# Split operands for the first two batches and ten slots of a fused attention and feed-forward kernel, other homes for batch 1's raw keys and values, another order of the first steps

## The chip, the cores and the metric

The kernel runs on one core of one Trainium2 chip. The metric is device time in microseconds (us) of the whole program; a result is the median over runs. About 0.2% (3.6 us) is what a measurement of this kernel can tell from no change.

The engines by their names in the profile: PE (TensorE, matmuls; PEld its weight loads), DVE (VectorE), ACT (ScalarE), POOL (GpSimd), SP (SyncE, here only a queue that issues DMA transfers).

## The reference

Three stages follow one another. Eight batches, eight heads, 576 rows, head dimension 64; 4608 tokens of width 512; hidden widths 2048 and 1536.

```python
k_p = k.reshape(B, H, 72, 8, D).mean(axis=3)
v_p = v.reshape(B, H, 72, 8, D).mean(axis=3)
scores = (1 / sqrt(D)) * q @ k_p.T
attn = softmax(scores)
x = attn @ v_p
h = x @ w_in
x = (h * cos(h)) @ w_out
out = (silu(x @ w_gate) * (x @ w_val)) @ w_out2
```

## The kernel before, in words

**Order of the work.** Attention for batch 0 comes first, as a written-out list of steps (`program`, line 1083). Then 9 blocks of 512 tokens go through the second stage in 16 slots each (a slot is 128 hidden columns); the steps of batches 1 to 7 are hung on those slots by hand (`START`, `MID`, `LATE`, `EXP`, `NORM`, lines 412 to 425). The third stage follows from about 995 us on and is not touched. A scheduler of the framework takes the instructions in priority of program order, by its own model of time, and lets later ones go ahead where earlier ones are not ready; on the chip each engine then runs its list strictly in that order.

**Number formats.** An fp32 matmul is one instruction that the trace shows as two records. The other form, fp32r, needs each operand as a high and a low part: the high part is made by a copy on ACT, the low part by a subtraction on DVE, and the product is hi\*hi + hi\*lo + lo\*hi, three matmuls. `ACTB = 2` (line 67) and `Y32 = NF1` = 16 (line 68) say where plain fp32 is used: for batches 0 and 1 in the attention product (`do_av`, line 375), and for all 16 slots of block 0 in the second product of the second stage (`pe_y`, line 591).

**Attention, per tile of 128 rows.** `do_qt` transposes q on PE; `do_s` (298) makes scores into two PSUM banks of the tag `att`, the minima on DVE (312) and the exponentials on ACT (318); `do_norm` (330) scales into `pm` on DVE (343, 350); `do_pt` (354) transposes `pm` on PE into an `att` bank and copies it to SBUF (363, 366); `do_av` multiplies with v, four head pairs per group of tiles, into `att` banks, and ACT moves the result into `ring` (399). The tag `att` has two banks. For batches 2 to 7 `do_pt` also makes low parts on DVE (369, 373), `do_norm` a copy of the leftover columns (352), `prep_v` the low parts of v (267 to 280), and `do_av` has five products per head pair in place of two.

**Weights.** All weights arrive as 64-bit numbers and are turned into fp32 by ACT (477) and three DVE operations (482, 487, 494); `w_in` pieces ("i", 16 of them) are split as well (1010, 994). `conv` (979) does it in a fixed list, the 8 first pieces of `w_in`, then `w_out` pieces ("o", 16) in turn with the other 8; `fill(m)` takes m steps from it. `load_i` and `load_o` issue the loads on SP's queue; o pieces pass through a ring of two buffers, i pieces land where the finished piece will be (`wa..`).

**Second stage, per slot.** `pe_h` (531): 12 matmuls of 512 columns. `turns` and `cosine` (542, 565): two DVE operations, three on ACT. `pe_y`: four fp32 matmuls, or 12 fp32r matmuls; for the latter `parts` (575) makes the split of the result (584, 587) and, in blocks 0 and 1, that of the `w_out` piece (553, 586).

**Raw keys and values.** Those of batch 1 (`load_kv1`, 189) go to places of later `w_in` pieces (tags `wa30` to `wa32`, `wa20` to `wa22`), are added up by DVE (steps K0, K1, K2, U0), and the loads of those pieces wait on SP's queue until then. Those of later batches are added up by POOL.

Of the kernel before, what the change touches and what calls it, by code (L numbers as in the profile page):

```python
# [8 lines left out]
F32 = mybir.dt.float32  # L9
F32R = mybir.dt.float32r  # L10
# [15 lines left out]
def fused_kernel(  # L26
# [18 lines left out]
    nc = tc.nc  # L45
    B, H, S, D = q.shape
# [3 lines left out]
    P = 128  # L50
    POOL = 8
    SP = S // POOL
    NP = H // 2
    SM = 64
    SL = SP - SM
    TB = 512
    NB = NT // TB
    KC = DM // P
    NF1 = FF1 // P
# [5 lines left out]
    PTW = 320  # L65
    LEAD = 4
    ACTB = 2
    Y32 = NF1

    const = ctx.enter_context(tc.tile_pool(name="const", bufs=1))  # L70
    chain = ctx.enter_context(tc.tile_pool(name="chain", bufs=2))
# [12 lines left out]
    mask = few[:, 0]  # L84
# [20 lines left out]
    kT = p1a.tile([P, NP, 2 * SP], F32, name="kT")  # L105
    av_tiles = {}

    def av_tile(nm, b):

        kind = F32 if b < ACTB else F32R  # L110
        if (nm, kind) not in av_tiles:
            shape = {"v": [P, NP, P], "p": [P, NP, PTW], "x": [P, PTW]}["x" if nm == "ptx" else nm[0]]
            t = av_tiles[nm, kind] = p1a.tile(shape, kind, name=f"{nm}_{b}", tag=nm)
            if nm in ("vmh", "vml", "vl2"):
                nc.gpsimd.memset(t if kind is F32 else t.bitcast(F32), 0.0)
        return av_tiles[nm, kind]

    nc.gpsimd.memset(kT, 0.0)
    for nm in ("vmh", "vml", "vl1", "vl2", "pth", "ptl", "ptx"):
        av_tile(nm, 0)  # L120

    def raw_tile(nm):
        return chain.tile([P, 2, TB], F32, name=nm, tag="raw", bufs=2)
# [64 lines left out]

    def load_kv1():

        for g in range(3):
            t = wts.tile([P, 2, TB], F32, name=f"k1_{g}", tag=f"wa3{g}")
            kraw1.append(t if g < 2 else t[: SL * NP])
            if g < 2:
                for x in range(2):
                    nc.sync.dma_start(t[x * SM : (x + 1) * SM], kview[1][g, x])
            else:
                for r in range(2):
                    nc.sync.dma_start(t[: SL * NP, r], kleft[1][r])
        for j in range(0, NP + 1, 2):  # L200
            t = wts.tile([P, 2, TB], F32, name=f"v1_{j}", tag=f"wa2{j // 2}")
            for r in range(2):
                rows = t[r * SM : (r + 1) * SM]
                if j < NP:
                    nc.sync.dma_start(rows, vview[1][r, :, j : j + 2])
                else:
                    nc.sync.dma_start(rows[:, 0], vleft[1])
            vraw1.append((j, t[:, : min(2, NP + 1 - j)]))

    def pool_sum(eng, dst, raw):  # L210
        h = POOL * D // 2
# [37 lines left out]
            nc.scalar.mul(to[:, :, SM:], ps[rows, 2 * P :].rearrange("d (s p) -> d p s", p=NP), -EXP_SCALE)  # L249

    def prep_v(b):
        vmh, vml, vl1, vl2 = (av_tile(nm, b) for nm in ("vmh", "vml", "vl1", "vl2"))
        vp = vps.pop(b)
        if b < ACTB:
            for r in range(2):
                rows, cols = slice(r * SM, (r + 1) * SM), slice(r * D, (r + 1) * D)
                nc.scalar.mul(vmh[rows, :, cols], vp[rows, :NP], 1.0 / POOL)
            nc.vector.tensor_mul(
                vl1[:SM].rearrange("q p (r d) -> q r p d", r=2),
                vp[:SM, NP : NP + 1].rearrange("q (a o) d -> q a o d", a=1).to_broadcast([SM, 2, NP, D]),  # L260
                mask[:SM].rearrange("q (p r o) -> q r p o", r=2, o=1).to_broadcast([SM, 2, NP, D]),
            )
            return
        for r in range(2):
            rows, cols = slice(r * SM, (r + 1) * SM), slice(r * D, (r + 1) * D)
            nc.scalar.mul(vmh[rows, :, cols], vp[rows, :NP], 1.0 / POOL)
            nc.vector.scalar_tensor_tensor(
                out=vml[rows, :, cols], in0=vp[rows, :NP], scalar=1.0 / POOL, in1=vmh[rows, :, cols],
                op0=ALU.mult, op1=ALU.subtract,
            )  # L270
        t = p1a.tile([P, H, SP], F32, name=f"vt_{b}", tag="e")[:, :, :D]
        nc.vector.tensor_mul(
            t, vp[:, NP : NP + 1].to_broadcast([P, H, D]), mask.rearrange("p (h o) -> p h o", o=1).to_broadcast([P, H, D])
        )
        t = t.rearrange("q (p r) d -> q r p d", r=2)
        h2 = vl1.rearrange("q p (r d) -> q r p d", r=2)
        l2 = vl2.rearrange("q p (r d) -> q r p d", r=2)
        for r in range(2):
            nc.scalar.copy(h2[:, r], t[:, r])
            nc.vector.tensor_sub(l2[:SM, r], t[:SM, r], h2[:SM, r])  # L280
# [49 lines left out]
    def do_norm(b, t, pm=None):  # L330
        n = TILES[t][1]
        e = es.pop((b, t))[:n]
        if b < ACTB:
            sm = sms.pop((b, t))[:n]
        else:
            sm = p1a.tile([P, H, 1], F32, name=f"sm_{b}_{t}", tag="sm", bufs=2)[:n]
            nc.vector.reduce_sum(sm[:, :, 0], e, axis=AX.X)
        nc.vector.tensor_scalar_add(sm, sm, 1e-9)
        nc.vector.reciprocal(sm, sm)
        if pm is None:  # L340
            pm = p1a.tile([P, H * SM + P], F32, name=f"pm_{b}_{t}", tag="pm")
        pms[b, t] = pm
        nc.vector.tensor_mul(
            pm[:n, : H * SM].rearrange("q (h s) -> q h s", h=H), e[:, :, :SM], sm.to_broadcast([n, H, SM])
        )

        for g in range(2):
            left = pm[:n, H * SM + g * SM : H * SM + (g + 1) * SM].rearrange("q (h s) -> q h s", h=H)
            if g == 0:
                nc.vector.tensor_mul(left, e[:, :, SM:], sm.to_broadcast([n, H, SL]))  # L350
            elif b >= ACTB:
                nc.vector.tensor_copy(pm[:n, H * SM + SM :], pm[:n, H * SM : H * SM + SM])

    def do_pt(b, t):
        pth, ptl, ptx = av_tile("pth", b), av_tile("ptl", b), av_tile("ptx", b)
        t0, n = TILES[t]
        o = t0 - GROUPS[GROUP[t]][0]
        pm = pms.pop((b, t))
        ps = psum.tile([P, NP, n], F32, name=f"pt_{b}_{t}", tag="att", bufs=2)
        for p in range(NP):  # L360
            pinned(nc.tensor.transpose(ps[:, p], pm[:n, p * P : (p + 1) * P], ident[:n, :n]), (b, t) == (0, 4))
        if b < ACTB:
            nc.scalar.copy(pth[:, :, o : o + n], ps)
            px = psum.tile([SM, n], F32, name=f"px_{b}_{t}", tag="att", bufs=2)
            nc.tensor.transpose(px, pm[:n, NP * P : NP * P + SM], ident[:n, :n])
            nc.scalar.copy(ptx[:SM, o : o + n], px)
            return
        nc.scalar.copy(pth[:, :, o : o + n], ps)
        nc.vector.tensor_sub(ptl[:, :, o : o + n], ps, pth[:, :, o : o + n])
        px = psum.tile([P, n], F32, name=f"px_{b}_{t}", tag="att", bufs=2)  # L370
        nc.tensor.transpose(px, pm[:n, NP * P :], ident[:n, :n])
        nc.scalar.copy(ptx[:, o : o + n], px)
        nc.vector.tensor_sub(ptx[SM:, o : o + n], px[SM:], ptx[SM:, o : o + n])

    def do_av(b, g, p):
        vmh, vml, vl1, vl2, pth, ptl, ptx = (
            av_tile(nm, b) for nm in ("vmh", "vml", "vl1", "vl2", "pth", "ptl", "ptx")
        )
        g0, n = (GROUPS if b else GROUPS0)[g]
        o = 256 if g == 2 else 0  # L380
        ps = psum.tile([P, n], F32, name=f"av_{b}_{g}_{p}", tag="att", bufs=2)
        terms = [
            (vmh, pth[:, p, o : o + n]),
            (vmh, ptl[:, p, o : o + n]),
            (vml, pth[:, p, o : o + n]),
            (vl1, ptx[:, o : o + n]),
            (vl2, ptx[:, o : o + n]),
        ]
        if b < ACTB:
            terms = [(vmh, pth[:, p, o : o + n])]  # L390
            terms += [(vl1[:SM], ptx[:SM, o : o + n])]
        for i, (w, x) in enumerate(terms):
            nc.tensor.matmul(ps, w[:, p], x, start=i == 0, stop=i == len(terms) - 1)  # L393
        t0 = b * S + g0
        done = 0
        while done < n:
            at = (t0 + done) % RING
            m = min(n - done, TB - at % TB)
            nc.scalar.mul(ring[:, p, at : at + m], ps[:, done : done + m], INV_2PI)
            done += m  # L400
# [549 lines left out]
    def load_i(m):  # L950
        for _ in range(m):
            u = next(to_load_i, None)
            if u is not None:
                _, j, c = order[u]
                cv_load(keys[u], w_in[c * P : (c + 1) * P, j * TB : (j + 1) * TB], f"wa{j}{c}")
# [62 lines left out]
    def fill(m):  # L1018
        for _ in range(m):
            conv_done[0] = next(conv_ops, len(order))  # L1020
# [26 lines left out]
        pool_sum(nc.vector, kps[0][:, 2 * g : 2 * g + 2], kst[:, 2 * g : 2 * g + 2])  # L1047
    pool_sum(nc.vector, kps[0][: SL * NP, NP:], kst[: SL * NP, NP:NK])
    prep_k(0)
    load_i(3)  # L1050
    load_kv1()
    fill(8)
    do_qt(0, 0)
    kfree = kst.rearrange("s h x -> s (h x)")
# [22 lines left out]
    def sum_v1():  # L1077
# [3 lines left out]


    program = (
        "s0 s1 f4 x0 s2 p0 V0 v x1 p1 f6 s3 s4 F3 a0 x2 p2 x3 p3 a1 w i1 q G2 K0 K1 K2 U0 X i11 o2 "
        "x4 b f6 "
    )
    steps = {
# [196 lines left out]
```

## Time and profile before

| what | value |
|---|---|
| median of 3 runs | 1787.25 us (1786.49 to 1788.84) |
| the profiled execution | 1786.07 us |
| its span, first to last instruction | 1784.3 us |
| mean granted clock of TensorE | 0.997 |

Outside the span lie 1.8 us. In all views times are us from the span's start. A timeline row is: start, length, engine, line, operation, out<-in, shape, count, and in square brackets the idle time of the engine just before with what ended it. Matmul records overlap: a record's length is longer than the step from one to the next. A row of the chain of waits gives start, length and what, without overlap, so there the length of a group is the time that it takes.

### The profile page before, as it was taken

The page shows a single profiled execution, that of the slowest core. Times are in us where ns is not written, and L with a number is a line of the kernel's source. Part 1 is how long each engine was busy: PE and PEld are TensorE (multiplying, and loading weights), DVE is VectorE, ACT ScalarE, POOL GpSimd, SP SyncE. Part 2 cuts the span into 40 slices and gives each one's busy share as a digit, 9 for nine tenths or more (in the row PEclk, how much of TensorE's full clock was granted, in tenths as well). Part 3 has the DMA queues.
Part 4 walks back from the last instruction along what each step waited for, and adds up shares of the span by engine and source line. Part 5 has one row for each costly group of instructions (what it writes and reads, how often), then busy time and mean ns, then how long its engine had stood idle before and what let it go on. Part 6 is the DMA issues. An engine that isn't in the chain of part 4 may idle for free.

```text
span 1784.3 us, 23241 instructions
## 1 busy us (share of the span) xinstructions
PE 1737.2 (97%) x8076; PEld 1444.5 (81%) x8076; DVE 1169.0 (66%) x2006; ACT 996.1 (56%) x1815; POOL 122.1 (7%) x217
## 2 busy tenths in 40 slices
PE   4979999999999999999999999999999999999998
PEld 3546588888888888888888778888888888999998
DVE  6695377867767677687675677853684377458346
ACT  5576477767667767677575565433443344344333
POOL 0131300403003011000000000000000000000000
PEclk9989999999999999999999999999999999999999
DMA  9553244646576455575775587675567657777772
GB/s 232 162 162 105 82 149 145 194 133 205 131 228 208 118 201 145 188 213 160 230 265 182 192 321 270 202 274 195 195 208 257 197 191 225 298 255 244 298 253 90
DMA packets 240244, 357.00 MB, mean 200 GB/s; under 512 B 141696, under 2 KB 147840, under 8 KB 240128
## 3 DMA queue, kind: packets, MB, share of 16 engines
q1 hardware_dynamic: 235440, 354.35, 61.5%
q10 hardware_dynamic: 4688, 1.18, 0.3%
q8 instruction: 64, 1.05, 0.2%
q14 instruction: 52, 0.43, 0.1%
HBM read 285.74 MB, written 69.73 MB: 199 GB/s over the span
## 4 chain that ended last, share of the span: by engine, by line
PE 89%; DMA 4%; DVE 4%; ACT 2%; issue 1%; POOL 0%; SPq 0%; ACTq 0%; DVEq 0%; POOLq 0%
PE X L791 14%; PE oX L921 8%; PE h L537 7%; PE h L538 7%; PE h L539 7%; PE acc L606 7%; PE Y L791 7%; PE acc L608 7%; PE acc L607 7%; PE oY L921 4%; PE av L393 3%; PE Z L791 3%; PE acc L599 2%; PE oZ L921 2%; PE s L308 2%; DMA w2r<-w_dram 1%
## 5 line engine op out<-in xcount | busy, mean ns | idle before, releaser
L791 PE MATMUL X<-t_P,wc 128*128 128x512 f32 (+1 forms) x1080 | 232.9, 368 | 2.3 <-ACT u L840 2.3
L537 PE MATMUL h<-xhl,wa 128*128 128x512 f32 x576 | 232.0, 403 | 1.3 <-DVE w L573 1.3
L539 PE MATMUL h<-xhl,wa 128*128 128x512 f32 x576 | 225.9, 392 | 0.0
L538 PE MATMUL h<-xhl,wa 128*128 128x512 f32 x576 | 225.9, 392 | 0.0
L791 PEld LDWEIGHTS X<-t_P,wc 128*128 128x128 f32 x1080 | 196.5, 188 | 29.1 <-ACT u L840 4.0
L606 PE MATMUL acc<-gh,wo_ring 128*128 128x512 f32 x448 | 179.3, 400 | 0.0
L607 PE MATMUL acc<-gl,wo_ring 128*128 128x512 f32 x448 | 174.8, 390 | 0.0
L608 PE MATMUL acc<-gh,wo_ring 128*128 128x512 f32 x448 | 174.8, 390 | 0.0
L547 ACT ACTIVATE w<-h,few 128x512 f32<-128x512 f32 x144 | 98.9, 687 | 121.3 <-PE h L539 121.0
L548 DVE SCALAR_TENSOR_TENSOR w<-w,h 128x512 f32<-128x512 f32 x144 | 98.2, 682 | 68.8 <-ACT w L547 68.5
L537 PEld LDWEIGHTS h<-xhl,wa 128*128 128x128 f32 x576 | 109.1, 189 | 27.8 <-issue 3.8
L573 DVE SCALAR_TENSOR_TENSOR w<-w,h 128x512 f32<-128x512 f32 x144 | 98.4, 683 | 49.9 <-ACT w L570 48.2
L538 PEld LDWEIGHTS h<-xhl,wa 128*128 128x128 f32 x576 | 108.9, 189 | 23.7 <-issue 2.4
L539 PEld LDWEIGHTS h<-xhl,wa 128*128 128x128 f32 x576 | 108.9, 189 | 23.0
L587 DVE TENSOR_TENSOR gl<-w,gh 128x512 fp32r<-128x512 f32 x128 | 90.9, 710 | 51.0 <-ACT gh L584 50.1
L584 ACT CAST gh<-w 128x512 fp32r<-128x512 f32 x128 | 78.9, 616 | 69.3 <-DVE w L573 47.3
L569 ACT ACTIVATE w<-w 128x512 f32<-128x512 f32 x144 | 91.1, 633 | 46.1 <-DVE w L548 45.1
L843 DVE TENSOR_TENSOR p<-p,X 128x512 f32<-128x512 f32 (+1 forms) x60 | 37.8, 632 | 116.8 <-PE X L791 108.6
L126 ACT CAST xhl<-pst 128x1024 fp32r<-128x1024 f32 (+1 forms) x70 | 67.7, 968 | 71.3 <-PE oX L921 26.1
L921 PE MATMUL oX<-xhl,wc 128*128 128x512 f32 (+1 forms) x480 | 102.7, 368 | 0.0
L608 PEld LDWEIGHTS acc<-gh,wo_ring 128*128 128x128 f32 x448 | 84.1, 188 | 18.6
L606 PEld LDWEIGHTS acc<-gh,wo_ring 128*128 128x128 f32 x448 | 84.2, 188 | 17.0 <-issue 0.8
(196 smaller groups left out, 3377.2 us busy)
## 6 DMA issues: line engine op xcount, KB each, us to landing
wc<-wc_dram SPq DMA_DIRECT2D x273, 512.0 KB
wo_ring<-wo_dram SPq DMA_DIRECT2D x112, 512.0 KB
wc_dram<-wc SPq DMA_DIRECT2D x42, 512.0 KB
wc_dram<-ow SPq DMA_DIRECT2D x42, 256.0 KB
y_dram<-yo SPq DMA_DIRECT2D x18, 512.0 KB
w_dram<-ce_w SPq DMA_DIRECT2D x36, 256.0 KB
st_i<-in_moe_w_in_dram SPq DMA_DIRECT2D x16, 512.0 KB
st_o<-in_moe_w_out_dram SPq DMA_DIRECT2D x16, 512.0 KB
```

Of the source, the lines that this page charges most:

```text
L537: nc.tensor.matmul(ps, whi, xhl[0][:, 0, c], start=c == 0, stop=False)
L538: nc.tensor.matmul(ps, whi, xhl[0][:, 1, c], start=False, stop=False)
L539: nc.tensor.matmul(ps, wlo, xhl[0][:, 0, c], start=False, stop=c == KC - 1)
L547: nc.scalar.activation(w, h, AF.Identity, bias=magic)
L548: nc.vector.scalar_tensor_tensor(out=w, in0=w, scalar=MAGIC, in1=h, op0=ALU.subtract, op1=ALU.subtract)
L569: nc.scalar.activation(w, w, AF.Sin, scale=PI)
L573: nc.vector.scalar_tensor_tensor(out=w, in0=w, scalar=1.0, in1=h, op0=ALU.subtract, op1=ALU.mult, reverse0=True)
L606: nc.tensor.matmul(acc[n][i], a[:, cols], xh, start=f == 0, stop=False)
L607: nc.tensor.matmul(acc[n][i], a[:, cols], xl, start=False, stop=False)
L608: nc.tensor.matmul(acc[n][i], b[:, cols], xh, start=False, stop=f == NF1 - 1)
L791: nc.tensor.matmul(ps[:, :hb], w, t[:, x, c, :hb], start=first and c == 0 and n == 0, stop=c == 1 and n == 2, skip_group_check=not first,)
L921: nc.tensor.matmul(banks[key][m][:, :hb], u, x[:, b, i, :hb], start=first_ and j == i == k == 0, stop=j == NJ - 1 and i == 1 and k == 2, s ...
```

## The change

The attention product of batches 0 and 1 takes the split path of the later batches (five fp32r products per head pair, low parts in `do_pt` and `prep_v`), and the tiles for it are allocated once. `Y32` becomes 6, so that slots 6 to 15 of block 0 take the split path of `pe_y`. Batch 1's raw keys and values go to the `wo` tiles of the second product, to two `wa` tiles, and to the `gh` and `gl` tiles, values in five pieces in place of three. Ten pieces of `w_in` are loaded behind batch 0's raws (four ahead of batch 1's raws, six behind) in place of three, batch 1's q follows them, and the first two o pieces and the last two i pieces take other places in the list of steps, in which scores 3 and 4, the fills and the first attention product also trade places.

```diff
-    Y32 = NF1
+    Y32 = 6
...
-    def av_tile(nm, b):
-        kind = F32 if b < ACTB else F32R
+    def av_tile(nm):
+        if nm not in av_tiles:
...
     def load_kv1():
-        for g in range(3):
-            t = wts.tile([P, 2, TB], F32, name=f"k1_{g}", tag=f"wa3{g}")
-            kraw1.append(t if g < 2 else t[: SL * NP])
...
+        for g in range(2):
+            t = p1w.tile([P, 2, TB], F32, name=f"k1_{g}", tag="wo", bufs=2)
+            kraw1.append(t)
+            for x in range(2):
+                nc.sync.dma_start(t[x * SM : (x + 1) * SM], kview[1][g, x])
+        t = wts.tile([P, 2, TB], F32, name="k1_2", tag="wa32")[: SL * NP]
...
-        for j in range(0, NP + 1, 2):
-            t = wts.tile([P, 2, TB], F32, name=f"v1_{j}", tag=f"wa2{j // 2}")
+        for j in range(NP + 1):
+            if j < NP:
+                t = chain.tile([P, 1, TB], F32, name=f"v1_{j}", tag="gh" if j < 2 else "gl", bufs=2)
+            else:
+                t = wts.tile([P, 2, TB], F32, name=f"v1_{j}", tag="wa33")[:, :1]
...
     def prep_v(b):
-        if b < ACTB:
...
-            return
...
     do_norm:
-            elif b >= ACTB:
+            else:
                 nc.vector.tensor_copy(pm[:n, H * SM + SM :], pm[:n, H * SM : H * SM + SM])
...
     do_pt:
-        if b < ACTB:
-            nc.scalar.copy(pth[:, :, o : o + n], ps)
-            px = psum.tile([SM, n], F32, name=f"px_{b}_{t}", tag="att", bufs=2)
-            nc.tensor.transpose(px, pm[:n, NP * P : NP * P + SM], ident[:n, :n])
-            nc.scalar.copy(ptx[:SM, o : o + n], px)
-            return
...
     do_av:
-        if b < ACTB:
-            terms = [(vmh, pth[:, p, o : o + n])]
-            terms += [(vl1[:SM], ptx[:SM, o : o + n])]
...
-    load_i(3)
+    load_i(4)
     load_kv1()
+    load_i(6)
+    load_q(1)
     fill(8)
...
-        "s0 s1 f4 x0 s2 p0 V0 v x1 p1 f6 s3 s4 F3 a0 x2 p2 x3 p3 a1 w i1 q G2 K0 K1 K2 U0 X i11 o2 "
+        "s0 s1 f4 x0 s2 p0 V0 v x1 p1 s3 f4 a0 x2 p2 s4 x3 p3 F3 a1 w o2 K0 K1 K2 U0 i2 G2 X "
         "x4 b f6 "
```

In the list of steps `s`, `x`, `p` are scores, normalisation and transposition of a tile, `a` the attention product of a group, `V`, `v` sums and preparation of v, `f`, `F`, `G` fills, `K`, `U` sums of batch 1, `i`, `o`, `q`, `b` loads, `X` the split of the first block.

## Rows read from the trace of the kernel before

**Rows 1.** The page's first line and its busy times.

```profile
span 1784.3 us, 23241 instructions
...
PE 1737.2 (97%) x8076; PEld 1444.5 (81%) x8076; DVE 1169.0 (66%) x2006; ACT 996.1 (56%) x1815; POOL 122.1 (7%) x217
```

**Rows 2.** Stretches: length, busy PE, PEld, DVE, ACT, POOL; clock, DMA, GB/s.

```profile
0.00:216.00 216.00, 176.29 (x596) 108.58 (x597) 132.74 (x254) 128.69 (x356) 47.84 (x87) 0.98 0.53 148
...
46.00:69.00 23.00, 21.47 (x43) 10.18 (x44) 11.44 (x31) 8.46 (x29) 0.00 (x0) 1.00 0.57 150
69.00:98.00 29.00, 20.24 (x97) 15.55 (x96) 22.82 (x42) 25.50 (x60) 7.22 (x9) 0.96 0.38 130
98.00:131.00 33.00, 28.71 (x90) 17.27 (x91) 29.73 (x49) 22.94 (x61) 15.00 (x21) 0.88 0.62 202
131.00:216.00 85.00, 85.00 (x297) 50.60 (x296) 39.65 (x71) 46.48 (x112) 21.18 (x39) 1.00 0.33 90
```

**Rows 3.** Chain of waits, batch 0's attention product and the first slot.

```profile
46.55 9.24 PE av L393 x16
...
59.36 9.27 PE av L393 x16
...
69.36 0.43 PE h L538
...
72.52 0.23 PE h L539
```

**Rows 4.** Timeline of PE: four places where it had waited, or was waited for.

```profile
43.34 2.43 PE L308 MATMUL s<-kT,qT 128*64 128x144 f32 x8 [2.20 <-ACT kst L318]
...
97.92 6.11 PE L599 MATMUL acc<-w,wo 128*128 128x512 f32 x8 [7.12 <-DVE wo L494]
...
117.23 1.14 PE L308 MATMUL s<-kT,qT 128*128 128x144 f32 x8
...
126.55 1.03 PE L293 MATMUL qp<-ident,q 128*128 128x128 f32 x4 [4.29 <-ACT e L318]
```

**Rows 5.** Chain of waits, later in block 0: fp32 products.

```profile
131.65 3.44 PE acc L599 x8
...
137.84 2.31 PE av L393 x8
...
191.36 2.74 PE av L393 x8
```

**Rows 6.** Chain of waits, attention product of later batches, split.

```profile
253.38 1.19 PE av L393 x10
...
495.17 2.99 PE av L393 x20
```

**Rows 7.** Groups by line, 216 to 500 us: what the split costs DVE.

```profile
L587 DVE TENSOR_TENSOR gl<-w,gh 128x512 fp32r<-128x512 f32 x44 | 31.2, 708 | 14.1 <-ACT gh L584 14.1
...
L586 DVE TENSOR_TENSOR wo<-wo,wo 128x512 fp32r<-128x512 f32 x14 | 9.6, 686 | 1.6 <-ACT wo L553 1.6
...
L369 DVE TENSOR_TENSOR ptl<-pt,pth 128x512 fp32r<-128x512 f32 x12 | 8.2, 683 | 0.0
...
L373 DVE TENSOR_TENSOR ptx<-px,ptx 64x128 fp32r<-64x128 f32 x12 | 3.5, 294 | 0.4
```

**Rows 8.** Timeline of SP's queue, first i and o loads.

```profile
37.45 17.07 SPq L470 DMA_DIRECT2D st_i<-in_moe_w_in_dram  x2
...
66.47 1.10 SPq L470 DMA_DIRECT2D st_o<-in_moe_w_out_dram  x2
```

**Rows 9.** Timeline of DVE, 96 to 123 us.

```profile
96.25 0.69 DVE L487 SCALAR_TENSOR_TENSOR wo<-st_o,wo 128x512 uint32<-128x512 uint32 x1
...
107.67 1.22 DVE L487 SCALAR_TENSOR_TENSOR wo<-st_o,wo 128x512 uint32<-128x512 uint32 x1
...
122.04 0.45 DVE L312 TENSOR_REDUCE mx<-s 128x4 f32<-128x288 f32 x1
```

**Rows 10.** Timeline of POOL, 107 to 109 us.

```profile
107.16 2.04 POOL L213 TENSOR_TENSOR kraw<-kraw 32x256 f32<-32x256 f32 x2
```

More of the change, by code (lines that the diff above doesn't have):

```diff
@@ L106, in fused_kernel @@
     av_tiles = {}
-    def av_tile(nm, b):
-        kind = F32 if b < ACTB else F32R
-        if (nm, kind) not in av_tiles:
+    def av_tile(nm):
+        if nm not in av_tiles:
             shape = {"v": [P, NP, P], "p": [P, NP, PTW], "x": [P, PTW]}["x" if nm == "ptx" else nm[0]]
-            t = av_tiles[nm, kind] = p1a.tile(shape, kind, name=f"{nm}_{b}", tag=nm)
+            t = av_tiles[nm] = p1a.tile(shape, F32R, name=nm)
             if nm in ("vmh", "vml", "vl2"):
-                nc.gpsimd.memset(t if kind is F32 else t.bitcast(F32), 0.0)
-        return av_tiles[nm, kind]
+                nc.gpsimd.memset(t.bitcast(F32), 0.0)
+        return av_tiles[nm]
     nc.gpsimd.memset(kT, 0.0)
     for nm in ("vmh", "vml", "vl1", "vl2", "pth", "ptl", "ptx"):
-        av_tile(nm, 0)
+        av_tile(nm)
     def raw_tile(nm):
@@ L189, in load_kv1 @@
     def load_kv1():
-        for g in range(3):
-            t = wts.tile([P, 2, TB], F32, name=f"k1_{g}", tag=f"wa3{g}")
-            kraw1.append(t if g < 2 else t[: SL * NP])
-            if g < 2:
-                for x in range(2):
-                    nc.sync.dma_start(t[x * SM : (x + 1) * SM], kview[1][g, x])
-            else:
-                for r in range(2):
-                    nc.sync.dma_start(t[: SL * NP, r], kleft[1][r])
-        for j in range(0, NP + 1, 2):
-            t = wts.tile([P, 2, TB], F32, name=f"v1_{j}", tag=f"wa2{j // 2}")
+        for g in range(2):
[4 more added lines that the diff above has]
+        t = wts.tile([P, 2, TB], F32, name="k1_2", tag="wa32")[: SL * NP]
+        kraw1.append(t)
+        for r in range(2):
+            nc.sync.dma_start(t[:, r], kleft[1][r])
+        for j in range(NP + 1):
+            if j < NP:
+                t = chain.tile([P, 1, TB], F32, name=f"v1_{j}", tag="gh" if j < 2 else "gl", bufs=2)
+            else:
+                t = wts.tile([P, 2, TB], F32, name=f"v1_{j}", tag="wa33")[:, :1]
             for r in range(2):
                 rows = t[r * SM : (r + 1) * SM]
[L204 to L208, printed above, removed]
+                nc.sync.dma_start(rows, vview[1][r, :, j : j + 1] if j < NP else vleft[1])
+            vraw1.append((j, t))
     def pool_sum(eng, dst, raw):
@@ L251, in prep_v @@
     def prep_v(b):
-        vmh, vml, vl1, vl2 = (av_tile(nm, b) for nm in ("vmh", "vml", "vl1", "vl2"))
+        vmh, vml, vl1, vl2 = (av_tile(nm) for nm in ("vmh", "vml", "vl1", "vl2"))
         vp = vps.pop(b)
-        if b < ACTB:
[L255 to L262, printed above, removed]
-            return
         for r in range(2):
@@ L350, in do_norm @@
                 nc.vector.tensor_mul(left, e[:, :, SM:], sm.to_broadcast([n, H, SL]))
-            elif b >= ACTB:
+            else:
                 nc.vector.tensor_copy(pm[:n, H * SM + SM :], pm[:n, H * SM : H * SM + SM])
     def do_pt(b, t):
-        pth, ptl, ptx = av_tile("pth", b), av_tile("ptl", b), av_tile("ptx", b)
+        pth, ptl, ptx = av_tile("pth"), av_tile("ptl"), av_tile("ptx")
         t0, n = TILES[t]
@@ L376, in do_av @@
         vmh, vml, vl1, vl2, pth, ptl, ptx = (
-            av_tile(nm, b) for nm in ("vmh", "vml", "vl1", "vl2", "pth", "ptl", "ptx")
+            av_tile(nm) for nm in ("vmh", "vml", "vl1", "vl2", "pth", "ptl", "ptx")
         )
```

## The prediction

> **What bounds the kernel now.** I read the page first: PE is busy for 97% of the span [rows 1], so what counts is PE's own work and the few places where it waits. The stretches say where those are: up to 216 us PE is busy for 176.3 of 216, and the change touches nothing behind that point, so the whole question lies in these 216 us [rows 2]. They fall into three stages. Up to 69 us batch 0's attention runs; its end is a chain on PE, two blocks of the attention product that each take about 9.25 us, then the first slot [rows 3]. The step from one 512-column matmul to the next is 0.43 us at 69 us and 0.23 us at 72.5 us [rows 3]: PE ran at the lower of its two levels (1.2 GHz) through these blocks and came to the upper one (2.4 GHz) in the first slot, although the column of the granted clock reads 1.00 there [rows 2]. I go by the spacing. From 69 to 131 us PE is not the bound: it waits 7.1 us for the first o piece and 4.3 us for batch 1's scores [rows 4], while DVE is busy for 22.8 of 29 us and then for 29.7 of 33 us [rows 2]. From 131 to 216 us PE is busy all the time and DVE for 39.7 of 85 us [rows 2]: there only less work on PE helps, and DVE has room.
>
> **The change, part by part.**
>
> *Slots 6 to 15 of block 0.* Four fp32 matmuls take 3.44 us [rows 5]; twelve fp32r matmuls at 0.23 us each [rows 3] take 2.76. That is 0.68 less per slot, 6.8 us for ten. These slots lie in the stage where PE is busy throughout, so I count all of it. The price is a copy of the weights and one of the result on ACT, which is busy for 46 of 85 us there, and two subtractions on DVE, 0.69 + 0.71 us per slot, 14 us in all [rows 7]: 39.7 + 14 of some 74 us that are left.
>
> *Batch 1's product.* Half a 256-column group takes 2.31 us, half a 320-column group 2.74 [rows 5]; split they take 1.19, and 2.99 for a whole one [rows 6]. Gains: 2 x (2.31 - 1.19) = 2.2 and 2 x 2.74 - 2.99 = 2.5, together 4.7 us, again where PE is busy throughout.
>
> *Batch 0's two blocks.* Split, a block is 20 matmuls of 256 columns. At the lower level 512 columns take 0.43 us [rows 3], so 20 x 0.215 = 4.3 in place of 9.25: 9.9 us for both. At the upper level it would be 2 x 1.19 [rows 6]; I take the lower, because the blocks that they replace ran there, and keep 3.8 us more as an end. The Trainium skill (TensorE: Matmul & The Clock Gate, Part 1: The HAM clock gate) has it that sustained activity brings the full clock; here 22 us with few gaps did not, so the measurement decides. By the page the sum would be those 3.8 us better.
>
> The group of 64 columns in slot 0 I count at nothing (0 to 1.5 us of gain; it has the same number of weight loads as the others, and they may set its pace).
>
> Sum of the PE work that goes: 6.8 + 4.7 + 9.9 = 21.4 us.
>
> *What the low parts add to the chain.* Before a block can run, the last tile's low parts must be there: a subtraction of 0.68 and one of 0.29 us on DVE [rows 7], behind the ACT copies. One such wait ahead of each block: -2 us. The ends are 0 (other work of PE fills it) and -4 (all four tiles pay, since the `att` bank is now held until DVE has read it too).
>
> *The order of scores 3 and 4, the first block and the fills.* Before, scores 4 and their 2.2 us wait stood ahead of the first block, 4.6 us in all [rows 4]; now they stand behind it and ahead of the last transposition. The first block starts earlier, but the second gets the wait. I take 0, ends -4.6 and +4.6.
>
> *Loads.* On SP's queue one i load stood 17 us behind the sums of batch 1, with q and all else behind it, and the o loads went out at 66.5 us [rows 8]. With other homes for the raws, six i loads and q go straight out, o behind them without a wait; only the last two i loads still wait for K2 and U0, and behind them stand batch 2's first raws, which the slots ask for from slot 17 on. The first o piece was turned by DVE at 96.3 us [rows 9], though its load went out 30 us earlier: the order had been laid out for a late load. With the load ahead, it can be turned before slot 2 needs it. Then the 7.1 us wait goes, and with it the slow product behind (6.1 us where 3.4 is usual [rows 4, 5], 2.7 us): +9.8. The other end is 0, if DVE's list still puts it late. I take all of it, because the charge for DVE comes next.
>
> *DVE between 69 and 131 us.* DVE gets, per batch, 4 x 0.68 + 0.4 of low parts, 5 x 0.29 of leftovers and as much for the copy of line 352, and for v five instructions of at most 0.68 less one of that size, about 1.6: 7.6 us [rows 7]. Batch 0's lie ahead of slot 0, where DVE idled 11.6 of 23 us [rows 2]; batch 1's sums stand in that same gap, which gets ten us shorter. Of batch 1's share three tiles and v fall in this stage, 1.6 + 3 x 1.3, with 0.9 for batch 0's last tile: 6.4 us on an engine with 9.5 us of idle time in 62. I charge all of it, -6.4; ends 0 and -6.4. Total on DVE: 132.7 [rows 2] + 15.2 + 14 = 162 us, to be done in about 216 - 22.8 = 193: it fits, at 84% of the time.
>
> Nothing else moves: the five sums of v in place of three pairs are the same elements, the memsets for batch 2 on POOL fall away, and PE is busy behind 216 us as before.
>
> **The sum.** 21.4 - 2 + 0 + 9.8 - 6.4 = 22.8 us less. The profiled execution took 1786.1 us (span 1784.3 and 1.8 around it): 1763.3. The median stands 1.2 above it: 1764.5 us.
>
> **The rivals.**
>
> *DVE becomes the bound of all of block 0.* For it: 162 us of work with its dependences, and 1.22 us for an operation that takes 0.69 otherwise [rows 9], while POOL was adding up raws [rows 10]. POOL is busy for 21 of the last 85 us [rows 2], so about 5 of the 20 new subtractions in slots 6 to 15 would be caught, 2.7 us. Against it: DVE is under half busy there. If it decides, what PE saves from slot 6 on (6.8 + 4.7) is lost in waits: 1764.5 + 11.5 = 1776. The Trainium skill (SBUF — State Buffer, Who interferes with whom) names this: a DVE instruction with two SBUF inputs contends with a GpSimd instruction that reads SBUF. The row agrees, and it speaks against lines 586 and 587.
>
> *The `att` banks become the bound (slower).* Place: `do_pt`, ten tiles. Each bank now waits for DVE as well as ACT, and DVE's list is long: at 117.2 us scores were made (1.1 us long), and DVE took them up at 122.04 [rows 4, 9], 3.7 us late. If every tile's low part came so late and PE had nothing else, ten tiles cost 37 us in place of the 2 counted: 1764.5 + 35 = 1799. It turns the sign once the lag exceeds (22.8 + 2) / 10 = 2.5 us per tile. Against it: in slots PE has 24 matmuls between two uses of `att`, and later batches run this path without a wait (behind 216 us PE is busy for 1737.2 - 176.3 of 1568 us [rows 1, 2], 7 us short).
>
> *More goes than I count.* DVE's charge is hidden, the blocks run at the upper level, and the 4.3 us wait goes too: 6.4 + 3.8 + 4.3 = 14.5 more, 1750.
>
> *It does nothing.* If the stage from 69 to 131 us is set by DVE and ACT alone, batch 0's gain is given back as a wait, and DVE's 6.4 and the waits eat the rest: around 1786.
>
> **How the numbers follow.** Forecast 0.60; DVE bound 0.18; more 0.13; `att` banks 0.05; nothing 0.04. The likeliest value is 1764.5. From the ends: best 21.4 + 1.5 + 3.8 + 4.6 + 9.8 = 41 less, worst 21.4 - 4 - 4.6 - 6.4 = 6.4 less; these need all terms to fall one way. I take 1750 (the third rival) to 1779 (the DVE rival and a little of the wait on `att`). About 0.2% (3.6 us) is what can be told from no change: faster 0.91, same 0.04, slower 0.05.
>
> **What would show it.** Attention blocks of batch 0 of some 4.3 us each in place of 9.25; the first slot at about 59 us in place of 68.6; no wait of 7 us ahead of the first L599; 2.8 us for the second product from slot 6 on; the end of block 0 at about 196 us in place of 219; from there on the two traces alike. Wrong would be: blocks that are shorter with a first slot no earlier; a wait of PE on L369 or L373; a DVE that is busy without a gap to the end of block 0 with PE waiting on L587.

## The result and the profile after

The changed kernel takes 1763.05 us (median; 1761.78 to 1763.69) against 1786.95 for the kernel before: ratio 0.9863, 95% interval 0.9846 to 0.9881, 23.9 us less. The forecast was 1764.5 in 1750 to 1779. The sum was right to 1.5 us; several of its terms were not, and their errors cancelled. One execution of `e1_y16` below took 4455 us and is left out of its median.

The page's first line and its busy times after:

```profile
span 1761.0 us, 23439 instructions
...
PE 1712.2 (97%) x8136; PEld 1451.3 (82%) x8136; DVE 1194.4 (68%) x2070; ACT 1008.8 (57%) x1839; POOL 126.7 (7%) x214
```

PE's busy time fell by 25.0 us and the span by 23.3 [rows 1], so PE idles 1.7 us longer than before. DVE's busy time rose by 25.4. The stretches of the changed kernel (length, busy PE, PEld, DVE, ACT, POOL; clock, DMA, GB/s), cut at its own first slot, first second product and later points:

```profile
60.00:63.00 3.00, 3.00 (x16) 2.79 (x14) 2.30 (x8) 2.59 (x6) 0.00 (x0) 0.50 1.00 358
63.00:84.20 21.20, 19.33 (x85) 15.74 (x85) 18.77 (x35) 19.34 (x51) 2.79 (x3) 0.81 0.10 33
...
98.00:116.00 18.00, 14.59 (x56) 8.73 (x55) 17.47 (x32) 13.93 (x35) 11.98 (x16) 1.00 0.47 147
...
123.50:143.00 19.50, 16.12 (x77) 11.64 (x76) 16.99 (x31) 14.85 (x38) 3.49 (x6) 1.00 0.44 151
143.00:197.00 54.00, 54.00 (x259) 44.52 (x258) 41.85 (x76) 43.92 (x100) 18.23 (x28) 1.00 0.36 93
```

PE loses time in the stretches from 63 to 84 us (1.9), 98 to 116 (3.4) and 123.5 to 143 us (3.4); from 143 us on it is busy throughout, as it was from 131 us on before [rows 2].

The chain of waits (start, length, what), the places that answer to [rows 3, 5]:

```profile
46.55 4.40 PE av L373 x20
...
58.38 4.65 PE av L373 x20
...
74.10 3.16 PE av L373 x17
77.26 2.08 PE s L297 x8
79.34 0.43 PE h L518
...
81.60 0.23 PE h L518
...
174.33 1.46 PE av L373 x10
```

Batch 0's two blocks take 4.40 and 4.65 us (9.24 and 9.27 before), and half a 320-column group of batch 1 takes 1.46 (2.74 before).

The timeline of PE at the points that mark the stages:

```profile
39.94 1.08 PE L350 MATMUL pt<-ident,vst 128*128 128x128 f32 x4 [6.15 <-DVE vst L339]
...
62.92 1.22 PE L517 MATMUL h<-xhl,wa 128*128 128x512 f32 x2
...
84.19 1.02 PE L579 MATMUL acc<-w,wo 128*128 128x512 f32 x2
...
113.20 0.50 PE L517 MATMUL h<-xhl,wa 128*128 128x512 f32 x1 [1.91 <-DVE w L553]
...
116.06 3.59 PE L579 MATMUL acc<-w,wo 128*128 128x512 f32 x8
...
126.01 0.39 PE L373 MATMUL av<-pth,vmh 128*128 128x256 f32 x1 [1.50 <-DVE ptl L352]
```

The first slot begins 5.7 us earlier (62.9 against 68.6; 59 had been forecast), the first second product 13.7 us earlier (84.2 against 97.9 [rows 4]), the fifth about 15.6 us earlier (116.1 against 131.65 [rows 5]). The rest of the 23.3 us, 7.7, is gained behind that point. No wait of 7 us stands ahead of the first L579, but other waits do. L352 is the line that was L369 before, the low part in `do_pt`. PE's waits from 60 to 215 us after (who for whom, us in total, times, longest):

```profile
PE h L517 <- DVE w L553: 2.5, 2, 1.9
PE qp L282 <- ACT e L307: 1.5, 2, 1.0
PE av L373 <- DVE ptl L352: 1.5, 1, 1.5
PE av L373 <- ACT qT L283: 1.2, 1, 1.2
PE s L297 <- DVE ptl L352: 1.0, 1, 1.0
PE av L373 <- ACT ring L379: 0.9, 1, 0.9
PE qp L282 <- DVE ptl L352: 0.7, 1, 0.7
```

They add up to 9.3 us, of which 3.2 wait for L352. Before it was 13.5, of which 11.4 lay in the two waits of [rows 4].

Ahead of the first slot it is the other way round. The stretch up to it, first in the kernel before, then in the changed one:

```profile
0.00:68.56 68.56, 41.90 (x115) 24.72 (x115) 40.54 (x93) 33.44 (x124) 4.43 (x18) 1.00 0.79 200
...
0.00:62.92 62.92, 30.38 (x123) 24.14 (x123) 44.94 (x113) 34.54 (x127) 3.52 (x16) 0.95 0.94 261
```

PE is busy 11.5 us less there and idles 5.9 more (32.5 against 26.7). From the first slot on, by these rows and the pages, it is busy 13.5 us less and idles 4.2 less.

### The profile page after: what moved, and what is told of

The parts are those of the page before. It is cut to its first block, busy times and chain, and to the rows that moved or that the text cites. A ratio compares the mean times of both kernels' runs of the same rounds, so it can differ in the third digit from the quotient of the medians.

```text
span 1761.0 us, 23439 instructions
## 1 busy us (share of the span) xinstructions
PE 1712.2 (97%) x8136; PEld 1451.3 (82%) x8136; DVE 1194.4 (68%) x2070; ACT 1008.8 (57%) x1839; POOL 126.7 (7%) x214
## 4 chain that ended last, share of the span: by engine, by line
PE 92%; DMA 3%; DVE 2%; ACT 2%; issue 0%; ACTq 0%; SPq 0%
PE X L771 16%; PE oX L901 8%; PE Y L771 8%; PE acc L586 7%; PE h L517 7%; PE acc L588 7%; PE acc L587 7%; PE h L518 7%; PE h L519 7%; PE oY L901 4%; PE Z L771 4%; PE av L373 3%; PE oZ L901 2%; PE s L297 2%; DMA st_i<-in_moe_w_in_dram 1%; PE pt L350 1%
## 5 line engine op out<-in xcount | busy, mean ns | idle before, releaser
L567 DVE TENSOR_TENSOR gl<-w,gh 128x512 fp32r<-128x512 f32 x138 | 96.7, 701 | 51.0 <-ACT gh L564 49.8
L517 PEld LDWEIGHTS h<-xhl,wa 128*128 128x128 f32 x576 | 108.6, 189 | 27.2 <-DVE w L553 4.6
L564 ACT CAST gh<-w 128x512 fp32r<-128x512 f32 x138 | 85.2, 618 | 70.3 <-DVE w L553 50.1
L586 PEld LDWEIGHTS acc<-gh,wo_ring 128*128 128x128 f32 x448 | 84.2, 188 | 16.9 <-issue 0.6
```

The source lines that it names most:

```text
L517: nc.tensor.matmul(ps, whi, xhl[0][:, 0, c], start=c == 0, stop=False)
L567: nc.vector.tensor_sub(b, w, a)
L586: nc.tensor.matmul(acc[n][i], a[:, cols], xh, start=f == 0, stop=False)
```

## The experiments

Twelve kernels, all timed against the kernel before on the same chip. Below, "less" is the difference to the median of the kernel before of that comparison. By the scatter of the executions on record (two standard errors), a difference between two of these kernels is good to about 2 us.

### Taking the parts away one by one

`e4_order_only` has the new loads, places and order, all of batches 0 and 1 and block 0 in fp32; `e3_b01_fp32` adds the split of slots 6 to 15, `e2_b0_fp32` that of batch 1 as well; the changed kernel adds batch 0.

```diff
 e4_order_only, against the changed kernel
-    Y32 = 6
+    Y32 = NF1
 and for batches 0 and 1, as before:
+    if b < SPB:   # in prep_v, do_norm, do_pt, do_av; SPB = 2
 e3_b01_fp32: Y32 = 6, SPB = 2
 e2_b0_fp32: Y32 = 6, SPB = 1
```

> Only the new loads, places of batch 1's raws and order of steps; batches 0 and 1 and all 16 slots in plain fp32. Theory (the wait for the first o piece goes with the earlier load, on its own): 1787 - 9.8 = 1777. Rival (the order only makes room for the splits, alone it moves nothing): 1785 to 1788.

> The changed kernel with batches 0 and 1 back in plain fp32; slots 6 to 15 split, loads and order as changed. Theory (terms add up with the order's 4.2 and the slots' 7.3): 1787 - 11.5 = 1775.5. Rival (the slots gain only where DVE has been relieved by an earlier start): 1780 or more.

> The changed kernel with batch 0 alone back in plain fp32 (its tiles are allocated again as fp32r for batch 1); batch 1, slots 6 to 15, loads and order as changed. Theory (the term of the two blocks stands by itself: 9.9 less 2 for the low parts): 1763 + 8 = 1771. Rival (the blocks' end sets when slot 0 begins, and with it when DVE comes to the first o piece, so that wait comes back too): 1763 + 8 + 7 = 1778, the first second product near 95 us.

Measured: 1782.83 (ratio 0.9977, 0.9968 to 0.9987), 4.2 less; 1776.08 (0.9948, 0.9935 to 0.9960), 10.8 less; 1773.03 (0.9926, 0.9914 to 0.9939), 13.9 less; the changed kernel 23.9 less. So the steps are, each good to about 2 us: order 4.2, slots 6.6, batch 1 3.1, batch 0 10.0.

The order brings less than half of the 9.8 that the prediction gave it. The timeline of PE in the order-only kernel, with a stretch of it (columns as in [rows 2]), shows what came instead:

```profile
80.11 0.50 PE L538 MATMUL h<-xhl,wa 128*128 128x512 f32 x1 [2.85 <-DVE w L574]
...
83.10 0.69 PE L394 MATMUL av<-pth,vmh 128*128 128x64 f32 x2 [1.09 <-ACT qT L295]
...
82.30:92.50 10.20, 9.40 (x29) 7.92 (x30) 6.02 (x12) 7.44 (x27) 0.00 (x0) 0.50 0.00 1
...
97.06 7.03 PE L600 MATMUL acc<-w,wo 128*128 128x512 f32 x16
```

The wait for the first o piece and the slow product behind it have gone, yet the first second product stands at 97.06 us, where it was 97.92 before: two other waits stand ahead of it, and behind them PE runs 10 us at its lower level (granted clock 0.50). In `e2_b0_fp32` it stands at 97.27, in `e3_b01_fp32` at 97.57, and the first is still 3 us better. When the first second product comes is no measure of the end. It also depends on what the scheduler puts ahead of it: 48 first-stage matmuls in these three kernels and before, 43 in the changed one. The rival of `e2_b0_fp32` had the place right (near 95), but the wait for the o piece did not come back, and the price was too high (7 us more).

Where batch 0's 10.0 comes from shows in part. The stretches at the lower level between 57 and 100 us, first in `e2_b0_fp32`, then in the changed kernel:

```profile
59.10:72.70 13.60, 13.60 (x29) 7.67 (x28) 8.49 (x21) 5.77 (x11) 0.00 (x0) 0.50 0.36 130
79.60:93.20 13.60, 13.33 (x41) 11.04 (x42) 8.99 (x18) 10.14 (x32) 2.02 (x4) 0.50 0.00 1
...
57.20:64.10 6.90, 5.78 (x24) 5.28 (x24) 5.76 (x14) 5.23 (x13) 0.00 (x0) 0.51 0.97 336
74.30:81.10 6.80, 6.80 (x28) 6.41 (x28) 4.84 (x10) 6.04 (x16) 0.00 (x0) 0.50 0.00 1
```

That is 27.2 us against 13.7. The first slot comes 4.2 us earlier by the split of batch 0 (62.9 against 67.1); behind it, less time at the lower level is part of what is left. What the rest is stays open.

The slots by themselves, from the other side:

> The changed kernel with Y32 back at 16, so that slots 6 to 15 of block 0 take four fp32 matmuls again; all else as changed. Theory (PE is the bound there): the 6.8 us of that term come back, 1763 + 6.8 = 1770. Rival (DVE is the bound of block 0, its 14 us of subtractions eat the gain): 1761 to 1765, no difference.

```diff
-    Y32 = 6
+    Y32 = NF1
```

Measured 1769.78 (0.9905, 0.9889 to 0.9920), 6.7 us above the changed kernel. Together with the 6.6 this is the term of 6.8. DVE is not the bound there.

### All splits, old order

```diff
-    load_i(4)
+    load_i(3)
     load_kv1()                # in its old form
-    load_i(6)
-    load_q(1)
...
-        "... x1 p1 s3 f4 a0 x2 p2 s4 x3 p3 F3 a1 w o2 K0 K1 K2 U0 i2 G2 X "
+        "... x1 p1 f6 s3 s4 F3 a0 x2 p2 x3 p3 a1 w i1 q G2 K0 K1 K2 U0 X i11 o2 "
```

> All splits, but the old loads, places of batch 1's raws and order of steps. Theory (terms add up: 21.4 of PE work less 2 for low parts less 6.4 for DVE): 1787 - 13 = 1774. Rival (without the order DVE gives all of it back as waits): 1785 or more. If the charge for DVE was wrong and it is hidden: 1768.

Measured 1766.04 (0.9882, 0.9869 to 0.9896), 21.0 less: the third case, and more. On top of the splits the order brings 3.0. Its second block and its first second product, on the timeline of PE:

```profile
58.95 0.28 PE L373 MATMUL av<-ptl,vmh 128*128 128x256 f32 x1
59.06 0.28 PE L373 MATMUL av<-pth,vml 128*128 128x256 f32 x1
...
83.34 3.70 PE L579 MATMUL acc<-w,wo 128*128 128x512 f32 x8 [0.89 <-DVE wo L474]
```

With the o loads going out at 66 us, as before, the 7.1 us wait is down to 0.9. So the load's place, which the prediction held responsible, is not needed for it to go.

That the 21.0 is close to the 21.4 of PE's work does not mean that the splits cost no waits. The second of batch 0's blocks ran at the upper level here (256 columns 0.11 us apart, 0.21 in the changed kernel), which the 21.4 does not count, and the slow product behind the o piece has gone. By the pages PE is busy 24.3 us less than before and idles 3.0 more. As 6.2 us of the wait for the o piece are gone, its other waits have grown by 9.2, where the prediction charges 2 + 6.4.

### Which piece of the order

> The changed kernel with the first two o loads moved back behind the split of the first block (step o2 after X), all else as changed. Theory (the load's place set the 7.1 us wait): that wait is back ahead of the first L579, 1763 + 9.8 = 1773. Rival (the wait went because the i pieces were loaded and turned earlier, which leaves DVE free in time): at most 1765, and the first second product still near 84 us.

```diff
-        "... a1 w o2 K0 K1 K2 U0 i2 G2 X "
+        "... a1 w K0 K1 K2 U0 i2 G2 X o2 "
```

Measured 1765.39 (0.9880, 0.9867 to 0.9893), 2.3 above the changed kernel, not 9.8. The first second product came at 87.9 us without a wait. But this edit tests little: it moved the loads by 3.5 us, to 59.6 us, and not back to 66.5 [rows 8], as the timelines of SP's queue show (the changed kernel, then this one):

```profile
56.16 1.09 SPq L450 DMA_DIRECT2D st_o<-in_moe_w_out_dram  x2
...
59.63 0.90 SPq L450 DMA_DIRECT2D st_o<-in_moe_w_out_dram  x2
```

The loads at their old time are tested by `e5_split_only` above and `e11_before_steps` below.

> The changed kernel with the old order of scores 3 and 4, fills and first attention product in the list of steps; loads and places as changed. Theory (the loads bring the 3 us that the order is worth on top of the splits): 1763. Rival (the steps bring them): 1766.

```diff
-        "... x1 p1 s3 f4 a0 x2 p2 s4 x3 p3 F3 a1 w ..."
+        "... x1 p1 f6 s3 s4 F3 a0 x2 p2 x3 p3 a1 w ..."
```

Measured 1766.72 (0.9893, 0.9877 to 0.9908), 3.7 above. That is the kernel with all splits and the old order within 0.7 us, so with the old steps the loads and places bring nothing that can be told. Its second block of batch 0 begins at 60.50 (58.38 in the changed kernel) and its first slot at 64.9 us (62.9).

> The kernel before with one edit: the first two o loads go out right behind the space for w_out (o2 behind w) in place of last. In the laid-out lists the first o piece moves from place 130 to 96 on DVE and the first second product from 110 to 95 on PE. Theory of the prediction (the wait for the first o piece is worth 9.8): 1787 - 9.8 = 1777. Rival (the wait goes, but what PE did ahead of it is late instead, so that most of it comes back as other waits, as in the run of the order alone): 1782 to 1787.

```diff
 against the kernel before
-        "... a1 w i1 q G2 K0 K1 K2 U0 X i11 o2 "
+        "... a1 w o2 i1 q G2 K0 K1 K2 U0 X i11 "
```

Measured 1780.57 (0.9964, 0.9952 to 0.9977), 6.0 less, between the two. Here the o piece does come forward: the first second product starts at 88.43 us with no wait. Of the 9.8 us that the wait and the slow product behind it had cost, 3.8 are given back. The timeline of PE shows a new wait that stands there instead, and behind it the scores at the lower level, with records of 2.12 us (1.14 at 117.23 us before [rows 4]):

```profile
81.51 0.43 PE L393 MATMUL av<-pth,vmh 128*128 128x64 f32 x2 [2.04 <-ACT ring L399]
...
83.31 2.12 PE L308 MATMUL s<-kT,qT 128*128 128x144 f32 x8
```

> The kernel before with only the order of scores 3 and 4, fills and first attention product changed; loads and places as before, no split. Theory (the steps bring what the order is worth, 4.2): 1783. Rival (alone they bring nothing, it takes the loads too): 1786 to 1788.

```diff
 against the kernel before
-        "... x1 p1 f6 s3 s4 F3 a0 x2 p2 x3 p3 a1 w i1 q ..."
+        "... x1 p1 s3 f4 a0 x2 p2 s4 x3 p3 F3 a1 w i1 q ..."
```

Measured 1784.98 (0.9991, 0.9982 to 1.0000), 1.6 less: between the two again, at the limit of what can be told. Here neither the o loads (65.8 us) nor the formats changed, and the wait for the first o piece has still gone down to 1.4; the waits for ACT have grown from 4.3 to 7.2. PE's waits from 60 to 215 us:

```profile
PE qp L293 <- ACT e L318: 7.2, 3, 3.9
PE acc L599 <- DVE wo L494: 1.4, 1, 1.4
```

Steps and o loads thus do not add up: 1.6 and 6.0 alone on the kernel before, 4.2 for the whole new order there, 3.0 on top of the splits. Each change lays out the engines' lists anew; that they draw on the same slack is argued from these sums, not shown.

What became of the wait shows in PE's time in the profiled executions (us, from the pages):

| kernel | span | PE busy | PE idle |
|---|---|---|---|
| before | 1784.3 | 1737.2 | 47.1 |
| `e11_before_steps` | 1783.9 | 1739.8 | 44.1 |
| `e7_before_o_early` | 1780.1 | 1738.2 | 41.9 |
| `e4_order_only` | 1778.3 | 1738.6 | 39.7 |
| `e5_split_only` | 1763.0 | 1712.9 | 50.1 |
| changed | 1761.0 | 1712.2 | 48.8 |

The first four run the same 8076 matmul records. With the wait gone PE idles 3.0, 5.2 and 7.4 us less than before, but it is busy 2.6, 1.0 and 1.4 us more, although the slow product is gone too: other matmuls run at the lower level, as in the two timelines above. The profiled execution of `e4_order_only` is the fastest of its ten, 2.9 us under its median; the others lie within 1.4 us of theirs.

### What more work for DVE costs

> The changed kernel with six more DVE subtractions of 128x128 (about 0.2 us each) behind each tile of batch 1, on a tile that nothing reads: some 7 us more for DVE, none for PE. Theory of the charge (DVE is the bound between slot 0 and slot 5, where three of the five tiles lie): 3 to 5 us more, 1766 to 1768. Rival (added work of DVE is hidden beside PE): 1763 to 1764.

```diff
+    extra = p1a.tile([P, P], F32, name="extra")
...
     do_pt, behind the last line:
+        if b == 1:
+            for _ in range(6):
+                nc.vector.tensor_sub(extra[:, :n], pth[:, 0, o : o + n].bitcast(F32), ident[:, :n])
```

Measured 1764.94 (0.9874, 0.9859 to 0.9890), 1.9 above the changed kernel. The added groups of DVE by line (shapes, count, busy, mean ns, idle before):

```profile
L359 DVE TENSOR_TENSOR extra<-pth,ident 128x128 f32<-128x128 f32 x24 | 8.6, 357 | 0.1
...
L359 DVE TENSOR_TENSOR extra<-pth,ident 128x64 f32<-128x64 f32 x6 | 2.2, 360 | 0.2
```

10.8 us of further instructions on DVE (its busy time on the page rose by 7.4) cost 1.9 us of time, with about 2 us of uncertainty: clearly less than one for one, and zero is not excluded. But the run says little on the stage in question. The added work lies between these times (duration ns min/median/max, first and last start):

```profile
L359 DVE TENSOR_TENSOR extra<-pth,ident x30: 224/284/864, 110.8 to 175.9; 128x128 f32<-128x128 f32 x24, 128x64 f32<-128x64 f32 x6
```

Only two of the five tiles, 5.2 of the 10.8 us, come before 143 us. The rest falls where DVE has room.

> The changed kernel with Y32 = 3, so that slots 3 to 5 of block 0 are split too. Theory of PE as the bound in all slots: 3 x 0.7 = 2.1 us less, 1761. Rival (in slots 3 to 5 DVE is the bound, each gets 1.4 us of subtractions): 1763 + 1 to + 4.

```diff
-    Y32 = 6
+    Y32 = 3
```

Measured 1763.23 (0.9873, 0.9859 to 0.9886), the same as the changed kernel. Neither expectation held: three more split slots neither bring the 2.1 us that PE saves nor cost more. The timeline of PE and two stretches of it show what takes up the saving:

```profile
109.41 0.80 PE L587 MATMUL acc<-gl,wo 128*128 128x512 f32 x1 [2.12 <-DVE gl L567]
...
118.85 0.50 PE L587 MATMUL acc<-gl,wo 128*128 128x512 f32 x1 [0.97 <-DVE gl L567]
...
109.40:112.80 3.40, 3.39 (x9) 2.81 (x10) 3.34 (x9) 2.88 (x6) 2.10 (x4) 0.50 0.50 181
123.10:126.50 3.40, 3.40 (x11) 2.71 (x11) 3.40 (x5) 2.71 (x15) 2.69 (x4) 0.50 0.35 99
```

PE waits 3.1 us in all for the low part that the split adds (L567), and twice it falls to the lower level, where the changed kernel has the upper one. PE's waits from 60 to 215 us add up to 8.8 us, no more than the 9.3 of the changed kernel; PE's busy time rose from 1712.2 to 1713.5 in place of falling by 2.1. In these slots DVE is busy nearly without a gap (17.47 of 18 us from 98 to 116 us in the changed kernel), and PE waits for it: the rival had the mechanism, but not the price.

> The changed kernel with POOL's sums of batch 2's raws hung two slots later in block 0. Theory of contention (operations of DVE are stretched while POOL adds, and DVE is what PE waits for up to slot 5): 1 to 3 us less, 1760 to 1762. Rival (what is stretched is hidden, or the stretched ones only move to later slots): 1763.

```diff
-                at(lates, START[b] + i + (b == 1), do_raw, b + 1, i)
+                at(lates, START[b] + i + 3 * (b == 1), do_raw, b + 1, i)
```

Measured 1762.55 (0.9864, 0.9851 to 0.9877), no difference that can be told from the changed kernel: the rival held. The Trainium skill (SBUF — State Buffer, Who interferes with whom) has a DVE instruction with two SBUF inputs contend with a GpSimd instruction that reads SBUF, and in the trace of the kernel before one such took 1.22 us in place of 0.69 [rows 9, 10]; moving POOL's sums two slots on is worth nothing here. How much contention in all costs was not tried.

None of the runs is clear of the changed kernel on the better side.

## Why the prediction came out right, step by step

**Slots 6 to 15: right.** Predicted 6.8, measured 6.6 and 6.7.

**Batch 0's blocks: right in size, and in the level of the clock.** 4.40 and 4.65 against 4.3 each. The net worth of splitting batch 0 is 10.0, where 9.9 less 2 for the low parts had been put; less time at the lower level behind the blocks is part of the difference.

**The low parts: a term that was too small.** -2, one wait ahead of each block. PE idles 5.9 us more ahead of the first slot. DVE has more to do ahead of tile 1's transposition, which starts at 39.94 us behind a wait of 6.15. The starts of the first block in the kernel with the order alone and in the one with the splits alone:

```profile
42.98 1.19 PE L394 MATMUL av<-pth,vmh 128*128 128x256 f32 x2 [1.73 <-ACT kst L319]
...
50.15 0.55 PE L373 MATMUL av<-pth,vmh 128*128 128x256 f32 x1 [0.78 <-issue]
```

Before and in the changed kernel it is 46.55. So the splits delay the first block by 3.6 us in either order, and the new order brings it forward by as much. The price of the order stands between the blocks, 7.4 us in place of 3.6: scores 4 stand there now. That the order gains ahead of the first block what it loses ahead of the second was forecast (term 0); the delay by the splits is what the -2 left out.

**Batch 1: not told apart from the forecast.** 4.7 of PE work, of which 3.1 arrive, good to about 2 us; PE's busy time falls by 4.3 from `e3_b01_fp32` to `e2_b0_fp32` (1733.8 and 1729.5 on the pages). In the changed kernel a wait of 1.5 us for L352 stands at 126.0 us, just where the 256-column group used to run without one.

**The order and the loads: the step that failed.** "Then the 7.1 us wait goes, and with it the slow product behind [...]: +9.8." The wait goes, but it is worth 4.2 with the whole order, 6.0 with the o loads alone, 3.0 on top of the splits, because other waits and other matmuls at the lower level take its place. Nor did the load's place decide: the wait is gone with the o loads alone, down to 1.4 with the steps alone, down to 0.9 with the splits alone. The order of steps, put at 0, is worth 1.6 alone and 3.7 in the changed kernel. (The 2.7 in this term sets a record's length, 6.11, against a step, 3.44; against a record of 3.6 it is 2.5.)

**The charge for DVE: the other mis-sized term.** -6.4, one for one, because DVE is busy for 29.7 of 33 us [rows 2]. It counted three tiles of batch 1 in that stage; the timeline of PE in the kernel before has the second one at its very end and the third behind it:

```profile
130.94 0.60 PE L361 MATMUL pt<-ident,pm 128*128 128x128 f32 x4
...
156.63 0.60 PE L361 MATMUL pt<-ident,pm 128*128 128x128 f32 x4
```

From the first slot on PE idles 4.2 us less. The wait for the o piece is 7.1 of that, so the other waits grew by 2.9, where 6.4 had been charged. That DVE can catch up later, since it was busy for only 39.7 of the next 85 us [rows 2], is argued, not shown; where it is busy without a gap, as in slots 3 to 5, `e8_y3` shows PE waiting for it.

**The group of 64 columns, counted at nothing,** costs PE 3.7 us (0.52 and 3.16 on the chain), where eight fp32 matmuls took 2.7 before (76.67 to 81.02 us, other work left out): it runs at the lower level; see below.

**The rivals.** DVE as the bound of all of block 0 did not come (slots 6 to 15 kept their gain). The lag on `att` banks is there, 3.2 us of PE's waits from 60 us on against the 35 of that rival. With it came one of the signs of being wrong that the prediction had named, a wait of PE on L369.

Set out by what PE did, forecast and measurement compare like this (us, changed kernel against the kernel before; the forecast from its terms 9.9, 2, 6.8 + 4.7 + 2.7 and 6.4 - 7.1):

| | busy, forecast | busy, measured | idle, forecast | idle, measured |
|---|---|---|---|---|
| ahead of the first slot | -9.9 | -11.5 | +2.0 | +5.9 |
| from the first slot on | -14.2 | -13.5 | -0.7 | -4.2 |
| in all | -24.1 | -25.0 | +1.3 | +1.7 |

The work that PE no longer does was counted well. The waits were not: 3.9 us too few ahead of the first slot, 3.5 too many behind it, and that these two cancel is luck. So is it that the order's 9.8 less the charge of 6.4 made 3.4, where 4.5 was measured (23.9 less the 19.4 that 21.4 and -2 leave).

## What to carry to other kernels

Removed work of the bounding engine can be counted at its full step from the trace where that engine is busy throughout and the second engine has slack: slots 6 to 15, with DVE busy for 41.85 of 54 us, kept their gain. Where the second engine is busy without a gap, the same edit brought nothing (slots 3 to 5). A wait on a list of work laid out ahead is worth less than its length: remove it and others appear, and the clock can fall elsewhere, so count the sum of all waits of the bounding engine and its busy time, not one wait. Where terms of opposite sign meet, a right total says little about each; undo the parts one by one, and compare busy and idle time stage by stage.

## What the runs showed of the hardware that was not expected

TensorE fell back to its lower level within slot 0. The step between 512-column matmuls was 0.23 us until about 70 us; then came transpositions, the 64-column group and waits of 0.7 and 1.2 us, and from about 74 us the 64-column matmuls stood 0.21 us apart, the scores took 2.08 us and 512 columns 0.43 us, until 81 us (chain above). The column of the granted clock reads 0.81 for 63 to 84 us and 0.50 for 74.3 to 81.1. In the first block of batch 0 the level rose only for the last three matmuls (from 0.21 to 0.11 us apart), though PE had worked without a gap in that block; the Trainium skill (TensorE: Matmul & The Clock Gate, Part 1: The HAM clock gate) lets one expect the upper level with sustained activity, and here the second block, 4.65 us long, stayed at the lower one; the upper one came in slot 0, at 64 us. With the old order and all splits the second block ran at the upper level (timeline of `e5_split_only` above), so the same block stands at either level in these kernels. The granted clock reads 0.50 for 60 to 63 us in the second block, and 1.00 for the fp32 blocks before [rows 2], whose successors show the lower level by their spacing [rows 3]. The trace's first clock record begins at 72.1 us there and at 50.4 us in the changed kernel, each time a rise; ahead of it the column reads 1.00 whatever the spacing says.
